# Token combinations of a seven-product pass: from GpSimd in one block to VectorE in eight pieces

## The chip, the cores and the metric

The kernel runs on one core of a Trainium2 chip. The metric is the device time of one execution in microseconds (us); lower is better. Engines are named as in the profile: PE (TensorE), DVE (VectorE), ACT (ScalarE), POOL (GpSimd), and SP, whose queue issues the DMAs.

## The reference

Eight batches of 576 tokens pass through Nystrom attention (8 heads of 64, 32 landmarks, an inverse found by six iterations) and then, all 4608 tokens, through a gated feed-forward layer with 512 inputs and 1536 hidden columns:

```
A, Bm, C = sm(q, k_lm), sm(q_lm, k_lm), sm(q_lm, k)
Z = 2 * Z - Z @ Bm @ Z            # six times
x = (A @ Z @ C @ v)               # heads side by side: 4608 x 512
xn = x / rms(x) * rms_g
out = (silu(xn @ w_gate) * (xn @ w_val)) @ w_out
```

## The kernel before

**Precision.** PE multiplies in a rounded 32-bit format, so operands are kept as a high part (a rounding copy, `Mhi`, `an[:,0]`, `h[:,0]`, `Bhi`) and a low part (the remainder, `Mlo`, `an[:,1]`, `h[:,1]`, `Blo`). A product takes three matmuls: high by high, high by low, low by high.

**Stage 1 (to about 514 us).** The hidden columns are halved into 12 blocks of 128; six (three pairs of gate and value blocks) belong to stage 1. For each batch i (a "chunk"), `mlp` makes 144 matmuls into the banks `psg` and `psv`, ACT takes the silu of one (L469, `s`), DVE multiplies with the other (L470, `s`), ACT makes the high part `h` (L474) and DVE the low part (L475); then `outs` adds the products of `h` with the output weights into `pso` and stores partial results. Into this stream of matmuls a `Mixer` slots the attention of later batches at fixed counts of matmuls: the two `front`s (one for each group of four heads) of batch i+2 (scores `sC` and `sA`, row maxima `mx` L576 to L579, exponentials `E` L582 and `eb` L586, transposes `tA`, landmark sums `lmT` L538), the steps of the inverse (matmuls `pn`, DVE `PV` L838 and `VF` L836), its weights (`W`, `WT`), and `second(b)` for batch i+1, which ends attention: its last piece scales the tokens (DVE `AT` L943), splits them (ACT `an` L945, DVE `an` L946), and forms what the seven-product pass will need.

**Token combinations.** For stage 2 each batch's tokens, cut in a 2 x 2 block of (feature half, token half), are written to the DRAM buffer `ad` as seven blocks with high and low part: three are blocks of `an`, four are differences. Before the change POOL makes the four differences (`tb`, L950 to L953), ACT their high parts in one cast (`thi`, L954), POOL the low parts in one subtraction of 128 x 1152 (L955), and two DMAs store them (L960, L961).

**Stage 2 (514 to 850 us).** For each batch `seven` makes for its six hidden blocks f the seven products of a fast 2 x 2 block scheme (`p<-xb,Bhi` and `p<-xb,Blo`): `step(f, n)` is product n, 12 matmuls, and what follows it on ACT and DVE (`u`, `vv`, `s`); `gate0`, `gate1` and `split` make `s` and `h` from them, on POOL for f up to 4 and on DVE for the last. `outs` for the other half of the output weights follows. `mix_blocks` prepares a pair's weights: two PSUM banks of mixed weights (`pM`) are summed to seven blocks, split into `Bhi` on ACT and `Blo` on DVE (three blocks, `lo1`) and POOL (four, `lo2`, L321). The last two products of a pass are issued inside `outs`, through the list `ends`.

**What sets the order.** Each engine runs its instructions in the order in which the program's scheduler puts them, with `tc.high_priority()` and `issue_after` moving a few; a wait blocks everything behind it on the same engine, and SP's DMA issues stand in one order too. Buffers come from tagged pools: a new tile of a tag waits for all readers of the tile whose slot it takes. `tb` and `thi` share the tag `sq`.

Of the kernel before, what the change touches and what calls it, by code (L numbers as in the profile page):

```python
# [55 lines left out]
def nystrom_moe_kernel(  # L56
# [237 lines left out]

    def mix_blocks(b, pair, banks):

        ps = mixed_banks(late, b, pair, banks)

        def sums():
            homes = HOMES[pair % NPAIR]  # L300
            hi = wp.tile([P, 7, 2, P], F32R, name="Bhi", tag=homes[0])
            if (b, pair) == (0, NPAIR + 1):
                lo1, lo2 = (mp.tile([P, n, 2, P], F32R, name=f"Blo{n}", tag="wraw", bufs=RAWS) for n in (3, 4))
            else:
                lo = wp.tile([P, 7, 2, P], F32R, name="Blo", tag=homes[1])
                lo1, lo2 = lo[:, :3], lo[:, 3:]
            s = lq.tile([P, 4, 2, P], F32, name="S7", tag="lraw", bufs=4)
            both = [p.rearrange("p (i z n) -> p z i n", i=2, z=2) for p in ps]
            a11, a21 = both[0][:, 0], both[0][:, 1]
            a12, a22 = both[1][:, 0], both[1][:, 1]  # L310
            kept(nc.scalar.copy(s[:, 2], a21))
            kept(nc.vector.tensor_add(s[:, 0], s[:, 2], a22))
            kept(nc.scalar.copy(hi[:, 0], a11))
            kept(nc.vector.tensor_sub(s[:, 1], s[:, 0], a11))
            kept(nc.vector.tensor_sub(s[:, 2], a11, s[:, 2]))
            kept(nc.scalar.copy(hi[:, 1:3], both[1]))
            kept(nc.vector.tensor_sub(s[:, 3], a12, s[:, 1]))
            kept(nc.vector.tensor_sub(lo1[:, 0], a11, hi[:, 0].bitcast(F32)))
            kept(nc.scalar.copy(hi[:, 3:], s))  # L319
            kept(nc.vector.tensor_sub(lo1[:, 1:3], both[1], hi[:, 1:3].bitcast(F32)))  # L320
            silu["mix"] = kept(nc.gpsimd.tensor_sub(lo2, s, hi[:, 3:].bitcast(F32)))  # L321
            blocks7[b, pair] = hi, lo1, lo2

        return sums

# [11 lines left out]

    later = []

# [7 lines left out]
    def seven(b, xb, between):  # L347
# [28 lines left out]
        def gate1(f):  # L376
# [3 lines left out]
            kept(eng.tensor_mul(s[:, 1], s[:, 1], vv[f][:, 1]))  # L380

        def gate0(f):
            kept(nc.vector.tensor_mul(ss[f][:, 0], ss[f][:, 0], vv[f][:, 0]))
# [7 lines left out]
        def step(f, n):  # L391
# [7 lines left out]
            elif n == 5:  # L399
                kept(nc.vector.tensor_copy(u[:, 2], p1))  # L400
                kept(nc.vector.tensor_add(v_[:, 1], u[:, 2], p7))
                if last:
# [3 lines left out]
            elif n == 2:  # L406
                kept(nc.vector.tensor_add(s[:, 0], u[:, 0], p2))
                if f > 1:
# [17 lines left out]
        for f in range(NF1):  # L426
            yield from between(f)
            new(f)
            second = ((1, 5), (0, 2)) if f > 1 else ((0, 2), (1, 5))
            for d, n in ((0, 1), *second, (0, 7), (0, 6), (1, 3), (1, 4)):  # L430
                if f >= d:
                    yield from step(f - d, n)
        yield from step(NF1 - 1, 5)
        ends.extend(step(NF1 - 1, n) for n in (3, 4))

# [42 lines left out]
    def outs(wts, b, f0, store, part, following, n0, after=2 * NF1):  # L478
# [5 lines left out]
        for at in range(0, len(groups), 2):  # L484
# [3 lines left out]
            for i, (t, n) in enumerate(order):  # L488
# [9 lines left out]
                yield MMO  # L498
                if ends:
                    yield from ends.pop(0)  # L500
# [13 lines left out]
    with tc.tile_pool(name="ap", bufs=1, side="right") as ap, tc.tile_pool(  # L514
# [180 lines left out]
        def rest(b, inverse, at):  # L695
# [27 lines left out]
            for n in range(6):  # L723
                yield from until(*next(at))
                with tc.high_priority():
                    newton_step(b, n)
                yield 0.45, 0.0
            yield from until(*next(at))
# [5 lines left out]
            for _ in range(4):  # L734
# [3 lines left out]
                if took:  # L738
                    yield took[0], 0.0
            stage["second"] = b  # L740

# [152 lines left out]
        def second(b):  # L894
# [49 lines left out]
            for g in range(2):  # L944
                nc.scalar.copy(an[:, 0, g], ATs[g])  # L945
                fixed["an", b] = nc.vector.tensor_sub(an[:, 1, g], ATs[g], an[:, 0, g].bitcast(F32))  # L946
            tb = ap.tile([P, 4, HS], F32, name="tb", tag="sq", bufs=2)
            thi = ap.tile([P, 4, HS], F32R, name="thi", tag="sq", bufs=2)
            (b11, b12), (b21, b22) = ((a[:, :HS], a[:, HS:]) for a in ATs)
            nc.gpsimd.tensor_sub(tb[:, 0], b12, b11)  # L950
            nc.gpsimd.tensor_sub(tb[:, 2], b22, b12)
            nc.gpsimd.tensor_sub(tb[:, 1], b22, tb[:, 0])
            nc.gpsimd.tensor_sub(tb[:, 3], b21, tb[:, 1])  # L953
            nc.scalar.copy(thi, tb)  # L954
            nc.gpsimd.tensor_sub(tb.bitcast(F32R), tb, thi.bitcast(F32))  # L955
            to = a_dram[b].rearrange("p (a n s) -> p a n s", a=2, n=7)
            af = an.bitcast(F32)
            nc.sync.dma_start(to[:, :, 0], af[:, :, 0, :HS])
            nc.sync.dma_start(to[:, :, 1:3].rearrange("p a n s -> p a (n s)"), af[:, :, 1])
            nc.sync.dma_start(to[:, 0, 3:], thi.bitcast(F32))  # L960
            nc.sync.dma_start(to[:, 1, 3:], tb)  # L961
            ans[b] = an

        hold = ctx.enter_context(ExitStack())
# [173 lines left out]
    def between(b, f):  # L1138
        if b == 0 and f == 1:
            later.append(mix_blocks(0, NPAIR + 2, (pg, "pg")))  # L1140
            yield 1.1
        if b == 0 and f == 2:
            later.pop(0)()

# [44 lines left out]
```

## Time and profile before

| | before |
|---|---|
| median of 3 runs | 851.82 us (851.22 to 851.9) |
| the profiled execution | 851.5 us, of which the span of the trace is 849.6 |
| PE, DVE busy | 801.3 us (94%), 605.3 us (71%) |
| ACT, POOL busy | 414.1 us (49%), 286.7 us (34%) |
| mean granted clock of PE | 0.968 of full speed |

PE is busy for all but 48.3 us of the span. A row of a timeline gives start, duration, engine, line, operation and tile, and in brackets the idle time of its engine before it with what ended that wait; "issue" there means that the profile shows no releaser.

### The profile page before, as it was taken

The page shows a single profiled execution, that of the slowest core. Times are in us where ns is not written, and L with a number is a line of the kernel's source. Part 1 is how long each engine was busy: PE and PEld are TensorE (multiplying, and loading weights), DVE is VectorE, ACT ScalarE, POOL GpSimd, SP SyncE. Part 2 cuts the span into 40 slices and gives each one's busy share as a digit, 9 for nine tenths or more (in the row PEclk, how much of TensorE's full clock was granted, in tenths as well). Part 3 has the DMA queues.
Part 4 walks back from the last instruction along what each step waited for, and adds up shares of the span by engine and source line. Part 5 has one row for each costly group of instructions (what it writes and reads, how often), then busy time and mean ns, then how long its engine had stood idle before and what let it go on. Part 6 is the DMA issues. An engine that isn't in the chain of part 4 may idle for free.

```text
span 849.6 us, 17802 instructions
## 1 busy us (share of the span) xinstructions
PE 801.3 (94%) x7012; PEld 629.9 (74%) x7012; DVE 605.3 (71%) x1295; ACT 414.1 (49%) x899; POOL 286.7 (34%) x274
## 2 busy tenths in 40 slices
PE   7878989899899899899899899899999999999997
PEld 5565657777678578578678587778788787979796
DVE  7999985856867847858857395767666757666662
ACT  4557555435345435435355485545455535444450
POOL 1034450320320411412303114555355535553650
PEclk9877989999999899999999999999999999999999
DMA  9855552350440620621345551052423233242412
GB/s 323 291 179 205 152 207 83 121 195 14 154 162 2 234 94 2 234 82 38 136 128 165 191 172 64 1 179 88 142 107 103 111 112 111 87 148 75 160 39 74
DMA packets 47715, 109.68 MB, mean 129 GB/s; under 512 B 4624, under 2 KB 19984, under 8 KB 47632
## 3 DMA queue, kind: packets, MB, share of 16 engines
q1 hardware_dynamic: 47632, 108.55, 37.3%
q8 instruction: 55, 0.90, 0.4%
q14 instruction: 28, 0.23, 0.1%
HBM read 73.14 MB, written 35.39 MB: 128 GB/s over the span
## 4 chain that ended last, share of the span: by engine, by line
PE 78%; DVE 6%; issue 5%; DMA 5%; ACT 3%; POOL 2%; SPq 0%; DVEq 0%; POOLq 0%; ACTq 0%
PE pso L111 32%; PE p L111 15%; PE psg L111 8%; PE psv L111 8%; PE pM L111 5%; DMA wrawv<-in_moe_w_val_dram 2%; PE pn L111 2%; PE sC L111 2%; PE pCV L111 1%; PE pss L111 1%; PE pO L111 1%; PE sA L111 1%; DMA wrawo<-in_moe_w_out_dram 1%; DMA xb<-ad 1%; DVE wgv L185 1%
## 5 line engine op out<-in xcount | busy, mean ns | idle before, releaser
L111 PE MATMUL pso<-wo,h 128*128 128x512 f32 x648 | 164.9, 407 | 3.0 <-DVE h L475 2.0
L111 PEld LDWEIGHTS pso<-wo,h 128*128 128x128 f32 x648 | 122.4, 194 | 37.8 <-issue 3.4
L111 PE MATMUL p<-xb,Bhi 128*128 128x288 f32 x672 | 139.7, 302 | 4.8 <-ACT u L396 3.8
L111 PE MATMUL pso<-lhio,h 128*128 128x512 f32 x432 | 140.2, 393 | 0.7 <-ACT h L387 0.5
L111 PEld LDWEIGHTS p<-xb,Bhi 128*128 128x128 f32 x672 | 107.4, 188 | 15.4 <-ACT u L396 6.9
L111 PEld LDWEIGHTS pso<-lhio,h 128*128 128x128 f32 x432 | 81.0, 188 | 24.7 <-issue 5.9
L111 PE MATMUL p<-xb,Blo 128*128 128x288 f32 x336 | 98.9, 294 | 0.0
L111 PE MATMUL psg<-an,Mhi 128*128 128x288 f32 x384 | 87.0, 310 | 5.3 <-ACT s L469 3.3
L111 PE MATMUL pso<-lloo,h 128*128 128x512 f32 x216 | 84.3, 390 | 0.0
L111 PE MATMUL psv<-an,Mhi 128*128 128x288 f32 x384 | 84.1, 303 | 0.0
L321 POOL TENSOR_TENSOR Blo<-S,Bhi 128x1024 fp32r<-128x1024 f32 x24 | 57.7, 2404 | 61.6 <-ACT Bhi L319 61.6
L111 PEld LDWEIGHTS psg<-an,Mhi 128*128 128x128 f32 x384 | 63.1, 193 | 18.5 <-ACT h L474 5.0
L389 POOL TENSOR_TENSOR h<-s,h 128x576 fp32r<-128x576 f32 x40 | 59.0, 1474 | 37.2 <-ACT h L387 37.2
L111 PEld LDWEIGHTS psv<-an,Mhi 128*128 128x128 f32 x384 | 62.9, 191 | 2.1
L111 PEld LDWEIGHTS p<-xb,Blo 128*128 128x128 f32 x336 | 63.1, 188 | 0.0
L469 ACT ACTIVATE s<-psg 128x288 f32<-128x288 f32 x96 | 39.5, 412 | 47.2 <-PE psg L111 46.9
L475 DVE TENSOR_TENSOR h<-s,h 128x576 fp32r<-128x576 f32 x48 | 51.5, 1072 | 12.8 <-ACT h L474 12.7
L111 PE MATMUL psv<-an,Mlo 128*128 128x288 f32 x192 | 59.0, 308 | 0.0
L111 PE MATMUL psg<-an,Mlo 128*128 128x288 f32 x192 | 58.9, 307 | 0.0
L387 ACT CAST h<-s 128x576 fp32r<-128x576 f32 x48 | 32.3, 672 | 54.5 <-POOL s L380 31.8
L1047 ACT COPY ob<-pso 128x512 f32<-128x512 f32 x36 | 21.1, 589 | 75.2 <-PE pso L111 43.7
L470 DVE TENSOR_TENSOR s<-s,psv 128x288 f32<-128x288 f32 x96 | 42.3, 446 | 20.7 <-PE psv L111 17.2
(172 smaller groups left out, 1558.7 us busy)
## 6 DMA issues: line engine op xcount, KB each, us to landing
xb<-ad SPq DMA_DIRECT2D x16, 1008.0 KB, 5.3
qk<-in_q_dram SPq DMA_DIRECT2D x16, 576.0 KB, 4.7
qk<-in_k_dram SPq DMA_DIRECT2D x16, 576.0 KB, 5.8
pd<-ob SPq DMA_DIRECT2D x36, 256.0 KB, 3.1
obl<-pd SPq DMA_DIRECT2D x36, 256.0 KB, 2.7
out_dram<-obl SPq DMA_DIRECT2D x36, 256.0 KB, 2.2
vt<-in_v_dram SPq DMA_DIRECT2D x16, 512.0 KB, 5.5
wrawg<-in_moe_w_gate_dram SPq DMA_DIRECT2D x12, 512.0 KB, 4.9
```

The source lines that it names most:

```text
L111: tc.keep_in_program_order(nc.tensor.matmul(*args, **kw))
L185: nc.vector.scalar_tensor_tensor(w, w, 3, wtail, op0=ALU.logical_shift_left, op1=ALU.bitwise_or)
L321: silu["mix"] = kept(nc.gpsimd.tensor_sub(lo2, s, hi[:, 3:].bitcast(F32)))
L387: kept(nc.scalar.copy(h[:, 0, TAIL:], s))
L389: kept(eng.tensor_sub(h[:, 1, TAIL:], s, h[:, 0, TAIL:].bitcast(F32)))
L469: silu["last"] = nc.scalar.activation(s[:, cols], banks[0], AF.Silu).ins
L470: nc.vector.tensor_mul(s[:, cols], s[:, cols], banks[1])
L475: gated[b, f0 // NF1, 2 * n + i] = nc.vector.tensor_sub(h[:, 1, TAIL:], s, h[:, 0, TAIL:].bitcast(F32))
L1047: nc.scalar.copy(ob, ps)
```

## The change

Three things are edited.

1. In `second(b)` the four POOL differences, the ACT cast, the POOL subtraction and the two 576 KB stores go. A generator `token_blocks` makes the same blocks as eight DVE instructions of 128 x 288 (four differences, L1000 of the changed kernel, and four low parts, L1005), four ACT casts of 128 x 288 (L1004) and eight stores of 144 KB (L1007). Its four pieces are taken one by one behind the steps of the **next** batch's inverse; those of the last batch right behind its own `an`. The tiles `t` come from the tag `tA` with three slots, so the fourth difference takes the slot of the first one, and waits for its two stores.
2. `mix_blocks` can hand out its sums in six pieces. Only batch 0's third pair uses that: a piece is taken behind each product n = 7 and n = 4 (f = 1 to 3), where before all sums came at the start of f = 2.
3. In each pass the addition `s = u + p2` of f = 1 is made right behind the copy of `u` for f = 0's product 5 (`first0`), and the two products in `ends` are issued one group of three `pso` matmuls later.

```
--- before.py
+++ after.py
@@ -292,11 +292,11 @@
     HOMES = [("wgv0", "wgv1"), ("wgv2", "wo0"), ("wo1", "wo2")]
     blocks7 = {}
 
-    def mix_blocks(b, pair, banks):
+    def mix_blocks(b, pair, banks, whole_pair=True):
 
         ps = mixed_banks(late, b, pair, banks)
 
-        def sums():
+        def sums(whole=True):
             homes = HOMES[pair % NPAIR]
             hi = wp.tile([P, 7, 2, P], F32R, name="Bhi", tag=homes[0])
             if (b, pair) == (0, NPAIR + 1):
@@ -308,20 +308,46 @@
             both = [p.rearrange("p (i z n) -> p z i n", i=2, z=2) for p in ps]
             a11, a21 = both[0][:, 0], both[0][:, 1]
             a12, a22 = both[1][:, 0], both[1][:, 1]
+            blocks7[b, pair] = hi, lo1, lo2
+
+            def high(n):
+                kept(nc.scalar.copy(hi[:, n], (a11, a12, a22)[n]))
+
+            def low(n):
+                kept(nc.vector.tensor_sub(lo1[:, n], (a11, a12, a22)[n], hi[:, n].bitcast(F32)))
+
             kept(nc.scalar.copy(s[:, 2], a21))
             kept(nc.vector.tensor_add(s[:, 0], s[:, 2], a22))
-            kept(nc.scalar.copy(hi[:, 0], a11))
+            yield
+            high(0)
             kept(nc.vector.tensor_sub(s[:, 1], s[:, 0], a11))
+            yield
             kept(nc.vector.tensor_sub(s[:, 2], a11, s[:, 2]))
-            kept(nc.scalar.copy(hi[:, 1:3], both[1]))
+            if whole:
+                kept(nc.scalar.copy(hi[:, 1:3], both[1]))
+            else:
+                high(1)
+            yield
             kept(nc.vector.tensor_sub(s[:, 3], a12, s[:, 1]))
-            kept(nc.vector.tensor_sub(lo1[:, 0], a11, hi[:, 0].bitcast(F32)))
-            kept(nc.scalar.copy(hi[:, 3:], s))
-            kept(nc.vector.tensor_sub(lo1[:, 1:3], both[1], hi[:, 1:3].bitcast(F32)))
+            if not whole:
+                high(2)
+            yield
+            low(0)
+            for n in (slice(0, 4),) if whole else (slice(0, 2), slice(2, 4)):
+                if n.start:
+                    yield
+                kept(nc.scalar.copy(hi[:, 3 + n.start : 3 + n.stop], s[:, n]))
+                if not whole:
+                    low(1 + n.start // 2)
+            if whole:
+                kept(nc.vector.tensor_sub(lo1[:, 1:3], both[1], hi[:, 1:3].bitcast(F32)))
             silu["mix"] = kept(nc.gpsimd.tensor_sub(lo2, s, hi[:, 3:].bitcast(F32)))
-            blocks7[b, pair] = hi, lo1, lo2
-
-        return sums
+
+        def at_once():
+            for _ in sums():
+                pass
+
+        return at_once if whole_pair else sums(False)
 
     def load_x(b):
         to = a_dram[b].rearrange("p (a n s) -> p a n s", a=2, n=7)
@@ -335,7 +361,7 @@
     def behind(ins):
         return tc.issue_after(ins) if ins else nullcontext()
 
-    later = []
+    later, pieces = [], []
 
     hs, ends = [], []
 
@@ -379,6 +405,9 @@
             silu["last"] = kept(nc.scalar.activation(s[:, 1], banks[f][0], AF.Silu))
             kept(eng.tensor_mul(s[:, 1], s[:, 1], vv[f][:, 1]))
 
+        def first0(f):
+            kept(nc.vector.tensor_add(ss[f][:, 0], us[f][:, 0], banks[f][1]))
+
         def gate0(f):
             kept(nc.vector.tensor_mul(ss[f][:, 0], ss[f][:, 0], vv[f][:, 0]))
 
@@ -398,13 +427,16 @@
                     gate1(f - 2)
             elif n == 5:
                 kept(nc.vector.tensor_copy(u[:, 2], p1))
+                if f == 0:
+                    first0(1)
                 kept(nc.vector.tensor_add(v_[:, 1], u[:, 2], p7))
                 if last:
                     gate1(f - 1)
                     gate0(f - 1)
                     split(f - 1)
             elif n == 2:
-                kept(nc.vector.tensor_add(s[:, 0], u[:, 0], p2))
+                if f != 1:
+                    first0(f)
                 if f > 1:
                     gate0(f - 2)
             elif n == 6:
@@ -430,6 +462,8 @@
             for d, n in ((0, 1), *second, (0, 7), (0, 6), (1, 3), (1, 4)):
                 if f >= d:
                     yield from step(f - d, n)
+                if pieces and n in (7, 4):
+                    next(pieces[0], None)
         yield from step(NF1 - 1, 5)
         ends.extend(step(NF1 - 1, n) for n in (3, 4))
 
@@ -496,7 +530,7 @@
                 yield MMO
                 mm(bank[t], hs[n][:, 1, sl], hi, start=False, stop=(n == NF1 - 1))
                 yield MMO
-                if ends:
+                if ends and i:
                     yield from ends.pop(0)
                 if n == NF1 - 1:
                     store(t, bank[t], obs.pop(t))
@@ -724,6 +758,7 @@
                 yield from until(*next(at))
                 with tc.high_priority():
                     newton_step(b, n)
+                next(blocks_of[b - 1], None)
                 yield 0.45, 0.0
             yield from until(*next(at))
             with tc.high_priority():
@@ -737,6 +772,9 @@
                     took = next(parts, None)
                 if took:
                     yield took[0], 0.0
+            if b == B - 1:
+                for _ in blocks_of[b]:
+                    yield -0.3
             stage["second"] = b
 
         def steady():
@@ -944,22 +982,41 @@
             for g in range(2):
                 nc.scalar.copy(an[:, 0, g], ATs[g])
                 fixed["an", b] = nc.vector.tensor_sub(an[:, 1, g], ATs[g], an[:, 0, g].bitcast(F32))
-            tb = ap.tile([P, 4, HS], F32, name="tb", tag="sq", bufs=2)
-            thi = ap.tile([P, 4, HS], F32R, name="thi", tag="sq", bufs=2)
-            (b11, b12), (b21, b22) = ((a[:, :HS], a[:, HS:]) for a in ATs)
-            nc.gpsimd.tensor_sub(tb[:, 0], b12, b11)
-            nc.gpsimd.tensor_sub(tb[:, 2], b22, b12)
-            nc.gpsimd.tensor_sub(tb[:, 1], b22, tb[:, 0])
-            nc.gpsimd.tensor_sub(tb[:, 3], b21, tb[:, 1])
-            nc.scalar.copy(thi, tb)
-            nc.gpsimd.tensor_sub(tb.bitcast(F32R), tb, thi.bitcast(F32))
             to = a_dram[b].rearrange("p (a n s) -> p a n s", a=2, n=7)
             af = an.bitcast(F32)
             nc.sync.dma_start(to[:, :, 0], af[:, :, 0, :HS])
             nc.sync.dma_start(to[:, :, 1:3].rearrange("p a n s -> p a (n s)"), af[:, :, 1])
-            nc.sync.dma_start(to[:, 0, 3:], thi.bitcast(F32))
-            nc.sync.dma_start(to[:, 1, 3:], tb)
+            blocks_of[b] = token_blocks(b, ATs, to)
             ans[b] = an
+
+        blocks_of = {}
+
+        def token_blocks(b, ATs, to):
+            (b11, b12), (b21, b22) = ((a[:, :HS], a[:, HS:]) for a in ATs)
+            ts = {}
+
+            def less(n, x, y):
+                ts[n] = ap.tile([P, 2, HS], F32, name=f"t{n}", tag="tA", bufs=TAB)
+                kept(nc.vector.tensor_sub(ts[n][:, 0], x, y))
+
+            def split(n):
+                t = ts[n]
+                nc.scalar.copy(t[:, 1].bitcast(F32R), t[:, 0])
+                kept(nc.vector.tensor_sub(t[:, 0].bitcast(F32R), t[:, 0], t[:, 1]))
+                for a in range(2):
+                    nc.sync.dma_start(to[:, a, 2 + n], t[:, 1 - a])
+
+            less(3, b22, b12)
+            less(1, b12, b11)
+            yield
+            split(3)
+            less(2, b22, ts[1][:, 0])
+            yield
+            split(1)
+            less(4, b21, ts[2][:, 0])
+            yield
+            split(2)
+            split(4)
 
         hold = ctx.enter_context(ExitStack())
 
@@ -1137,10 +1194,8 @@
 
     def between(b, f):
         if b == 0 and f == 1:
-            later.append(mix_blocks(0, NPAIR + 2, (pg, "pg")))
+            pieces.append(mix_blocks(0, NPAIR + 2, (pg, "pg"), False))
             yield 1.1
-        if b == 0 and f == 2:
-            later.pop(0)()
 
     mix.fill(mlp(early, B - 1, 0, ans.pop(B - 1), keep, lambda t: None, first_blocks))
     for b in range(B):
```

**On DVE, at the inverse of batch 6 in chunk 5.** `PV` are the steps of the inverse (L838 before, L876 after), `s` and `h` the gate of the running chunk. Before:

```order
L838 SCALAR_TENSOR_TENSOR PV<-PV,pn 128x192
L470 TENSOR_TENSOR s<-s,psv 128x288
L838 SCALAR_TENSOR_TENSOR PV<-PV,pn 128x192 x2
L470 TENSOR_TENSOR s<-s,psv 128x288
L838 SCALAR_TENSOR_TENSOR PV<-PV,pn 128x192
L475 TENSOR_TENSOR h_754<-s,h_754 128x576
L836 SCALAR_TENSOR_TENSOR VF<-PV,pn 128x128 x2
L470 TENSOR_TENSOR s<-s,psv 128x288 x2
```

The same place in the changed kernel, with buffer numbers (`t_4792` is the third difference, `t_4794` the first, `t_4821` the second, `t_4848` the fourth), up to the fourth difference:

```order
L876 SCALAR_TENSOR_TENSOR PV<-PV,pn 128x192
L1000 TENSOR_TENSOR t_4792<-AT 128x288
L1000 TENSOR_TENSOR t_4794<-AT 128x288
L504 TENSOR_TENSOR s<-s,psv 128x288
L876 SCALAR_TENSOR_TENSOR PV<-PV,pn 128x192
L1005 TENSOR_TENSOR t_4792<-t_4792 128x288
L1000 TENSOR_TENSOR t_4821<-AT,t_4794 128x288
L876 SCALAR_TENSOR_TENSOR PV<-PV,pn 128x192
L1005 TENSOR_TENSOR t_4794<-t_4794 128x288
L504 TENSOR_TENSOR s<-s,psv 128x288
L876 SCALAR_TENSOR_TENSOR PV<-PV,pn 128x192
L509 TENSOR_TENSOR h_744<-s,h_744 128x576
```

Behind these rows come the fourth difference (`t_4848`), the two `VF`, the last two low parts, the two `s`, and then `W` and `WT`. The eight new instructions stand between the steps of the inverse, at most two behind one `PV`.

**On ACT, at the end of chunk 5.** Before, the cast `thi` stands ahead of the cast of the chunk's last `h` and of the second front's exponentials (table load, `E`, `eb`):

```order
L945 CAST an<-AT 128x576 x2
L469 ACTIVATE s<-psg 128x288
L954 CAST thi<-tb 128x1152
L474 CAST h_1310<-s 128x576
L582 ACT_TABLE_LOAD
L582 ACTIVATE E,ss<-sC,mx 128x288 x2
```

After:

```order
L983 CAST an<-AT 128x576 x2
L503 ACTIVATE s<-psg 128x288
L508 CAST h_1324<-s 128x576
L616 ACT_TABLE_LOAD
L616 ACTIVATE E,ss<-sC,mx 128x288 x2
```

Only `thi` is gone; nothing takes its place there.

**On POOL, in the first pass of stage 2.** `Blo` is the low part of four blocks of one pair (three pairs), `s` and `h` are gate and split of f = 0, 1, 2. Before:

```order
L321 TENSOR_TENSOR Blo<-S_6428,Bhi 128x1024
L321 TENSOR_TENSOR Blo_6480<-S_6481,Bhi 128x1024
L321 TENSOR_TENSOR Blo<-S_6589,Bhi 128x1024
L380 TENSOR_TENSOR s_6526<-s_6526,vv 128x288
L389 TENSOR_TENSOR h_754<-s_6526,h_754 128x576
L380 TENSOR_TENSOR s_6558<-s_6558,vv 128x288
L389 TENSOR_TENSOR h_896<-s_6558,h_896 128x576
```

After:

```order
L344 TENSOR_TENSOR Blo<-S_6540,Bhi 128x1024
L344 TENSOR_TENSOR Blo_6592<-S_6593,Bhi 128x1024
L406 TENSOR_TENSOR s_6638<-s_6638,vv 128x288
L418 TENSOR_TENSOR h_744<-s_6638,h_744 128x576
L406 TENSOR_TENSOR s_6670<-s_6670,vv 128x288
L418 TENSOR_TENSOR h_886<-s_6670,h_886 128x576
L344 TENSOR_TENSOR Blo<-S_6689,Bhi 128x1024
```

The third pair's `Blo` has moved behind gate and split of the first two blocks.

## Rows read from the trace of the kernel before

**Rows 1.** The page: busy time by engine, share of the span, instructions.

```profile
PE 801.3 (94%) x7012; PEld 629.9 (74%) x7012; DVE 605.3 (71%) x1295; ACT 414.1 (49%) x899; POOL 286.7 (34%) x274
```

**Rows 2.** The chain in time order, chunks 1 and 5: start, us, what.

```profile
166.56 2.27 issue
...
171.34 1.59 PE pso L111 x6
...
398.21 0.93 PE pso L111 x4
...
400.33 6.12 PE pso L111 x26
406.44 2.29 issue
...
411.84 2.56 PE pso L111 x6
```

**Rows 3.** Timelines of DVE, ACT and POOL at the end of chunk 5.

```profile
398.46 2.64 DVE L946 TENSOR_TENSOR an<-AT,an 128x576 fp32r<-128x576 f32 x2
...
403.57 2.77 DVE L475 TENSOR_TENSOR h<-s,h 128x576 fp32r<-128x576 f32 x1 [0.98 <-ACT h L474]
...
407.32 2.57 DVE L538 TENSOR_REDUCE lmT<-qk 128x64 f32<-128x1152 f32 x2
...
401.80 1.16 ACT L954 CAST thi<-tb 128x1152 fp32r<-128x1152 f32 x1 [3.51 <-POOL tb L953]
...
407.02 1.28 ACT L582 ACT_TABLE_LOAD   x1 [3.49 <-DVE mx L579]
...
403.04 2.68 POOL L955 TENSOR_TENSOR tb<-tb,thi 128x1152 fp32r<-128x1152 f32 x1 [1.27 <-ACT thi L954]
```

**Rows 4.** All instructions of L475: duration in ns, min/median/max.

```profile
L475 DVE TENSOR_TENSOR h<-s,h x48: 717/753/2766, 55.7 to 511.1; 128x576 fp32r<-128x576 f32 x48
```

**Rows 5.** Windows: PE, PEld, DVE, ACT, POOL busy, PEclk, DMA share, GB/s.

```profile
406.00:410.00 4.00, 1.10 (x6) 0.20 (x6) 4.00 (x10) 2.63 (x7) 0.00 (x0) 1.00 0.37 147
410.00:414.00 4.00, 4.00 (x44) 2.93 (x44) 3.54 (x13) 0.55 (x2) 0.33 (x1) 0.57 0.00 0
```

**Rows 6.** Timelines of PE and DVE at the end of chunk 6.

```profile
468.48 0.73 PE L111 MATMUL pso<-wo,h 128*128 128x512 f32 x2 [1.01 <-ACT h L474]
471.22 1.49 PE L111 MATMUL pso<-wo,h 128*128 128x512 f32 x4 [2.01 <-DVE h L475]
472.63 1.96 PE L111 MATMUL pM<-wgv,WT 64*32 64x512 f32 x16
...
468.46 2.71 DVE L475 TENSOR_TENSOR h<-s,h 128x576 fp32r<-128x576 f32 x1 [2.98 <-ACT h L474]
```

**Rows 7.** Timelines in chunk 0: ACT, PE, DVE.

```profile
111.21 1.15 ACT L954 CAST thi<-tb 128x1152 fp32r<-128x1152 f32 x1 [2.92 <-POOL tb L953]
...
114.32 1.17 PE L111 MATMUL sC<-qk,lmT 64*32 64x288 f32 x2 [1.15 <-ACT E L582]
...
49.50 3.12 DVE L188 SCALAR_TENSOR_TENSOR wgv<-wrawg,wgv 128x512 int32<-128x512 int32 x1
```

**Rows 8.** DVE timeline through the inverse in chunk 5.

```profile
434.29 0.35 DVE L838 SCALAR_TENSOR_TENSOR PV<-PV,pn 128x192 f32<-128x192 f32 x1
435.19 0.45 DVE L470 TENSOR_TENSOR s<-s,psv 128x288 f32<-128x288 f32 x1 [0.54 <-PE psv L111]
435.88 0.35 DVE L838 SCALAR_TENSOR_TENSOR PV<-PV,pn 128x192 f32<-128x192 f32 x1 [0.24 <-PE pn L111]
```

**Rows 9.** DMA issues by tile: count, KB each, us from issue to landing.

```profile
ad<-an SPq DMA_DIRECT2D x8, 288.0 KB, 2.8
```

**Rows 10.** The first pass of stage 2: timelines of PE and POOL.

```profile
537.73 0.54 PE L111 MATMUL p<-xb,Bhi 128*128 128x288 f32 x2 [1.86 <-ACT u L396]
...
541.89 0.53 PE L111 MATMUL p<-xb,Bhi 128*128 128x288 f32 x2 [0.64 <-ACT u L396]
...
537.46 2.40 POOL L321 TENSOR_TENSOR Blo<-S,Bhi 128x1024 fp32r<-128x1024 f32 x1 [7.90 <-ACT Bhi L319]
```

## The prediction

> **What bounds the kernel now.** I read the page first: PE is busy for 801.3 of 849.6 us [rows 1], no other engine for more than 71%. So the time is PE's own work plus the stretches in which PE waits, and the change, which gives PE no more and no less to multiply, can only act through those 48.3 us and through what a wait does to PE's clock. Next I followed the chain that ended last, to see where PE waits: the same place returns in chunks 1 to 5, at the second front. In chunk 5 PE ends its `pso` products at 406.44, is idle for 2.29 us, makes the first two `sC`, waits again, and is back at `pso` at 411.84 [rows 2]. The first front of the same batch, the same work with nothing to wait for, took from 399.14 (398.21 + 0.93) to 400.33, 1.19 us [rows 2].
>
> Then I looked at what the other engines did in those microseconds [rows 3]. DVE makes `h` (L475) in 2.77 us; the same instruction has a median of 0.753 and a minimum of 0.717 [rows 4]. It runs from 403.57 while POOL's subtraction of 128 x 1152 runs from 403.04 to 405.72, and ends at 406.34, 0.62 us after that. `an`, beside POOL's differences, takes 2.64 us for two, while two at the shortest would take about 1.45 (twice L475's 0.72, the same shape and kind). And `h` started late: ACT's high part of `h` stands behind the cast `thi`, which waited 3.51 us for POOL's differences. Behind `h` come the first group's row maxima, then ACT's table load at 407.02 (idle 3.49 us for `mx`) and the exponentials, and DVE's `lmT`, 407.32 to 409.89; PE's second front needs both. So the stall is made by the token combinations: once through the queue on ACT, once through DVE's slowness beside POOL.
>
> By the Trainium skill ("SBUF — State Buffer", Who interferes with whom) a DVE instruction with two SBUF inputs and a GpSimd instruction that reads SBUF exclude each other for their whole length. By that rule `h` would end at 405.72 + 0.72 = 406.44; the trace has 406.34, so it agrees, and bears on the first rival below.
>
> **Term 1: second fronts of chunks 1 to 5.** What the stall costs is the time from the end of `pso` to the next `pso`, less 1.19, and what the lowered clock adds to the next six `pso` (26 took 6.12 us, so six take 1.41). Chunk 5: 411.84 - 406.44 - 1.19 = 4.21, and 2.56 - 1.41 = 1.15: 5.4 us. Chunk 1: 171.34 - 166.56 - 1.19 = 3.59, and 0.18: 3.8 [rows 2]. Chunks 2 to 4, worked out alike, give 4.8, 6.5 and 5.3. Sum 25.8. The granted clock is 1.00 in the 4 us around the idle time, and 0.57 in the 4 us after it [rows 5]: what is lost to the clock follows the wait, and goes with it.
>
> Does all of it go? With POOL silent, and `thi` gone, in chunk 5: `an` ends near 399.9 instead of 401.1 (1.45 for 2.64), two `s`, `mx` and `tA` take DVE to about 401.5; ACT makes its part of `h` by 401.3, DVE its own by 402.3, the maxima follow to about 403.0, `lmT` takes 2.57 as before, to 405.6; ACT's table load (1.28) and exponentials end near 405.3. PE arrives at 406.44. Margin 0.8 us: the whole stall goes. If I am 1 us wrong in every chunk, 0.2 to 1 us of it comes back in each. **25.8**, bounds 21 and 26.
>
> **Term 2: end of chunk 6.** PE waits 1.01 us for ACT's `h` and 2.01 for DVE's (2.71 long) [rows 6]. Behind it four `pso` take 1.49 us (0.94 at 6.12 for 26) and the 16 `pM` 1.96 (twice the 1.0 that they take elsewhere at full clock). Sum 4.5. Here the last batch's own eight instructions stand around this `h`: six DVE instructions at 0.45 ahead of what follows it, two or four of them ahead of `h` itself, some 1.8 us, in place of POOL's 4 us; I put `h` at 466.5 to 467, PE needs it from 467.47. **4.5**, bounds 2 and 5.
>
> **Term 3: chunk 0.** At 111.21 `thi` stands ahead of the table load, waiting 2.92 us for POOL; PE waits at 114.32 for `E` [rows 7]. The cast ends at 112.36, and the table load follows; without it the load waits for `mx` alone, at about 108.7 by the shorter `an`: 3.7 us earlier, `lmT` (2.57 long, to about 111.3) and `E` are both there by 111.4, and I add 0.6 for a clock that I expect to recover only partly. Earlier in chunk 0 DVE's work stands without idle time and POOL's combinations lengthen it by about 4 us, as I read it (one weight instruction of 3.12 us [rows 7] carries 2.4 of them); 3.6 us of new work come back in the next inverse. Net 1.3. **5.6**, bounds 3 and 8.
>
> **Term 4: the new instructions.** Per batch eight DVE instructions of 128 x 288. The trace has no such subtraction with POOL silent; the nearest row is `s`, the same size, 0.45 us [rows 8]: 3.6 us a batch, for 7 batches in the next inverse. Its steps are 1.59 us apart (434.29, 435.88) and PV takes 0.35; with two new instructions and an `s` behind a PV there are 0.35 + 0.9 + 0.45 = 1.70, 0.1 too many, elsewhere 1.25. The idle time there is 0.54 and 0.24 in one step [rows 8]. Bounds 0 (all in idle time) and 3.6 a batch (none); I take 0.15, nearer to the first by the idle rows: **-1.0**, bounds 0 and -7 (1 us a batch). The four ACT casts, about 0.4 each by size, lie in idle ACT time (49% busy). Behind the new instructions on DVE stand `VF`, `s`, `W` and `WT`, and PE waits for those.
>
> The fourth difference waits for the stores of the third block. In the times of the trace, the third's low part would end at 435.88 + 0.35 + 0.45 = 436.7; a store of 288 KB lands in 2.8 us [rows 9], so the slot is free at 439.5, and the fourth difference stands behind a PV of about 439.1 and an `h` of 0.75: 440.2. No wait, margin 0.7.
>
> By the Trainium skill ("DMA: Bandwidth & Descriptors", Anatomy of one DMA) each DMA pays about 2.0 us fixed, whatever its size, which speaks against eight small stores in place of two. By its fit 144 KB take about 2.3 us (an estimate), and 288 KB 2.7 against 2.8 in the trace; no row here shows stores of 144 KB. The slot would be free at 439.0, and the sum is the same, unless the stores run one behind the other (third rival).
>
> **Term 5: third pair of batch 0.** PE's idle time in the first pass, 1.86, 0.64 and two of 0.22, 2.9 us in all, is laid to the sums made in one block [rows 10]. Spread out, each piece sits ahead of some `u`, `vv` or silu for which the next product waits; I count four waits of 0.45 to 0.7, 2.5 us. And POOL's `Blo` now stands behind the second block's split: cast, 1.4 us of split, 2.40 us of `Blo` [rows 10], while the third block's products come; that I put at 3.2. Net **-2.8**, bounds -5 and +2.9.
>
> **Term 6.** The shifted `ends` and `first0`: single waits of 0.1 to 0.2 us a pass. **-0.6**, bounds -1.6 and +1.
>
> **Sum.** 25.8 + 4.5 + 5.6 - 1.0 - 2.8 - 0.6 = 31.5. 851.5 - 31.5 = 820.0, for a profiled execution 0.3 below the median of the runs shown, so 820 stands for either.
>
> **Rivals.**
> *The stall goes only by half*: what delays the front is DVE's own queue, and the next in line (`lmT`, `E`) ends 2.5 us late in each chunk. For it: the margin of 0.8 us comes out of a chain of seven durations. Against: L475's length, and POOL's end 0.62 us before its end. 820 + 13 = 833.
> *DVE becomes the bound in the inverse*: 3.6 us a batch, half of them not hidden, 7 batches: 12.6 - 1.0 more, 832. Against: the idle time in [rows 8], and DVE's 71% of the span [rows 1].
> *Stores one behind the other*: the third block's second store is the third in the queue. At 2.3 us each (which the page gives), or 2.8 each as in [rows 9], it lands near 442.5 to 444; the fourth difference, and DVE behind it, waits 2.3 to 3.7 us in six batches, 14 to 22 us: 834 to 842.
> *Slower*: the same wait, if a store takes so long that PE loses more than the 31.5 us: from 5.3 us in each of six batches, a landing of about 8.8 us instead of 2.8. At 7 us: 862. Against: [rows 9].
> *The third pair's spreading gains*: its stall goes, 2.9 instead of -2.8, and chunk 0 is at its upper bound: 812.
>
> **How the numbers follow.** Forecast (815 to 827) 0.62; spreading gains 0.12; half 0.09; DVE bound 0.07; stores 0.05; within 0.2% (1.7 us, about what a measurement of this kernel can tell from no change) 0.02; slower 0.03. The predicted time is 820. The range 811 to 834 leaves out the slower cases, most of the store rival and a rest of the best one, together under 0.2.
>
> **What would show it.** In the changed profile: no idle PE before the second `sC` of chunks 1 to 5, six `pso` behind it in about 1.41; L475 at a maximum under 1 us; `an` near 0.72; the clock at 1.00 there. Term 4 is wrong if PE waits for `PV`, `VF` or `W`, or if the fourth difference has idle time before it; term 5 is right if PE waits in the first pass for `Blo` of the third pair. The prediction falls if PE's waits at the fronts stay, with DVE or ACT busy with something else.

## The result and the profile after

| | before | after |
|---|---|---|
| median | 851.52 us (4 runs) | 819.36 us (4 runs, 819.07 to 819.86) |
| ratio to before | | 0.9625, 95% interval 0.9608 to 0.9641 |
| span of the profiled execution | 849.6 us | 818.1 us |
| mean granted clock | 0.968 | 0.985 |

Faster by 32 us, with 820 forecast. The page's first part, against [rows 1]: PE has 19 us less busy time for the same 7012 matmuls, POOL 60 us less. PE's idle time went from 48.3 to 35.9 us; so of the 31.5 us by which the span is shorter, 12.4 are waits that are gone, and 19.1 are time that the matmuls themselves no longer take.

```profile
PE 782.2 (96%) x7012; PEld 623.8 (76%) x7012; DVE 598.0 (73%) x1360; ACT 418.1 (51%) x925; POOL 226.4 (28%) x234
```

The chain at the second fronts of chunks 1 and 5, against [rows 2] (start, us, what):

```profile
157.00 6.12 PE pso L111 x26
...
164.30 1.59 PE pso L111 x6
...
375.05 0.93 PE pso L111 x4
...
377.16 6.12 PE pso L111 x26
...
384.46 1.59 PE pso L111 x6
```

No idle time stands between the 26 `pso` (to 383.28) and the next six: the second front takes 1.18 us, as the first one does (375.98 to 377.16). Chunk 5's six `pso` take 1.59 instead of 2.56; I had forecast 1.41, but chunk 1 took 1.59 before too. How a wait also lengthens the matmuls behind it shows in the kernel before: the same `sC` in the first front of chunk 5 and, behind the stall, in the second, where [rows 5] has a clock of 0.57.

```profile
399.61 0.40 PE L111 MATMUL sC<-qk,lmT 64*32 64x288 f32 x1
...
410.51 0.68 PE L111 MATMUL sC<-qk,lmT 64*32 64x288 f32 x1
```

Timelines of DVE and ACT at the end of chunk 5, against [rows 3]:

```profile
374.67 1.42 DVE L984 TENSOR_TENSOR an<-AT,an 128x576 fp32r<-128x576 f32 x2
...
377.56 0.76 DVE L509 TENSOR_TENSOR h<-s,h 128x576 fp32r<-128x576 f32 x1
...
379.30 2.57 DVE L572 TENSOR_REDUCE lmT<-qk 128x64 f32<-128x1152 f32 x2
...
376.85 0.67 ACT L508 CAST h<-s 128x576 fp32r<-128x576 f32 x1 [1.72 <-DVE s L504]
...
379.01 1.28 ACT L616 ACT_TABLE_LOAD   x1 [1.49 <-DVE mx L613]
...
381.44 0.20 ACT L620 ACTIVATION_READ_ACCUMULATOR eb<-sC,mx 128x1 f32 x1
```

`an` takes 1.42 for 2.64, `h` 0.76 for 2.77, and ACT's part of `h` waits for DVE's `s` and no longer behind `thi`. `lmT` ends at 381.87 and `eb` at 381.64; PE comes at 383.28, a margin of 1.4 us in this chunk. The clock in the windows there, against [rows 5] (the column behind POOL):

```profile
380.00:384.00 4.00, 4.00 (x45) 2.91 (x48) 2.47 (x6) 1.63 (x7) 0.00 (x0) 1.00 0.00 0
384.00:388.00 4.00, 4.00 (x50) 2.35 (x35) 3.88 (x14) 2.35 (x9) 1.24 (x2) 1.00 0.18 66
```

The end of chunk 6, timelines of PE and DVE, against [rows 6]: `pso` run through, `h` is done at 438.66, and the fourth difference waits 2.90 us for the stores of the third block, with nothing behind it that PE needs soon.

```profile
432.30 8.35 PE L111 MATMUL pso<-wo,h 128*128 128x512 f32 x36
440.57 1.09 PE L111 MATMUL pM<-wgv,WT 64*32 64x512 f32 x16
...
437.90 0.76 DVE L509 TENSOR_TENSOR h<-s,h 128x576 fp32r<-128x576 f32 x1
...
441.94 0.46 DVE L1000 TENSOR_TENSOR t<-AT,t 128x288 f32<-128x288 f32 x1 [2.90 <-DMA ad<-t]
```

Both traces hold all 7012 matmuls. But for `sC` and `sA` inside the second fronts, and the shifted products in `ends` in stage 2, they stand in one order. So what was gained up to a place is read from the same matmul in both: its start before less its start after is the "lead" of the changed kernel there.

| matmul | before | after | lead |
|---|---|---|---|
| a `pM` of the opening, after 42 us | 42.28 | 43.32 | -1.0 |
| `pso` behind the second front of chunk 0 (timeline) | 116.32 | 114.77 | 1.6 |
| the same, chunk 1 (chain) | 171.34 | 164.30 | 7.0 |
| the same, chunk 5 (chain) | 411.84 | 384.46 | 27.4 |
| two batches of `pM` at the end of stage 1 | 513.70 | 480.47 | 33.2 |
| 48 `pM` behind the first pass of stage 2 | 593.66 | 562.88 | 30.8 |
| last `pso` | 845.46 | 813.98 | 31.5 |

### The profile page after: what moved, and what is told of

Its sections match the earlier page's. It is cut to its first block, busy times and chain, and to the rows that moved or that the text cites. A ratio compares the mean times of both kernels' runs of the same rounds, so it can differ in the third digit from the quotient of the medians.

```text
span 818.1 us, 18012 instructions
## 1 busy us (share of the span) xinstructions
PE 782.2 (96%) x7012; PEld 623.8 (76%) x7012; DVE 598.0 (73%) x1360; ACT 418.1 (51%) x925; POOL 226.4 (28%) x234
## 4 chain that ended last, share of the span: by engine, by line
PE 83%; DVE 8%; issue 3%; ACT 2%; DMA 2%; POOL 1%; SPq 0%; DVEq 0%; POOLq 0%; ACTq 0%
PE pso L111 36%; PE p L111 14%; PE psg L111 9%; PE psv L111 9%; PE pM L111 5%; PE pn L111 2%; PE sC L111 2%; PE pCV L111 1%; PE pss L111 1%; PE pO L111 1%; DMA qk<-in_k_dram 1%; DMA vl<-in_vl_dram 1%; PE sE L117 1%; PE pW L111 1%; DVE u L429 0%
## 5 line engine op out<-in xcount | busy, mean ns | idle before, releaser
L111 PE MATMUL pso<-wo,h 128*128 128x512 f32 x648 | 158.5, 396 | 0.8 <-DVE s L504 0.8
L111 PEld LDWEIGHTS pso<-wo,h 128*128 128x128 f32 x648 | 118.6, 188 | 32.4 <-ACT E L616 4.2
L111 PEld LDWEIGHTS p<-xb,Bhi 128*128 128x128 f32 x672 | 109.2, 190 | 12.1 <-ACT u L425 2.8
L649 POOL TENSOR_TENSOR tA<-tA,mA 128x576 f32<-128x576 f32 x16 | 18.8, 1194 | 169.0 <-DVE mA L648 169.0
L1165 DVE TENSOR_TENSOR obl<-obl,pso 128x512 f32<-128x512 f32 x36 | 24.6, 684 | 40.6 <-PE pso L111 40.5
```

Source lines behind the costliest of these rows:

```text
L111: tc.keep_in_program_order(nc.tensor.matmul(*args, **kw))
L649: nc.gpsimd.tensor_sub(tA, tA, mA.unsqueeze(2).broadcast_to([P, NB, M]))
L1165: kept(nc.vector.tensor_add(ob, ob, ps))
```

## The experiments

Times are medians; "lead" is read as in the table, for the same matmuls.

**The token combinations alone.** The changed kernel with edits 2 and 3 undone.

```
-            pieces.append(mix_blocks(0, NPAIR + 2, (pg, "pg"), False))
+            later.append(mix_blocks(0, NPAIR + 2, (pg, "pg")))
...
-                if ends and i:
+                if ends:
...
+                first0(f)
```

Expected: 

> Only the token combinations are changed (pieces on VectorE behind the next inverse); the third pair's sums, first0 and ends are as before. Theory, by the ledger of PE's checkpoints in the two traces (lead of the changed kernel 33.2 us at the end of stage 1, 30.8 after the first pass, 31.5 at the end): the combinations are worth 33.2, the other two edits lose 1.7 together. So 851.5 - 33.2 = 818.3. Rival: the other edits help the gain somewhere in stage 1 or take nothing: 819.4 or above.

Measured: 815.61 us, ratio 0.9578 (0.9564 to 0.9593). Its lead at the end of stage 1 is 35.1 against 33.2, and the 1.9 between them are there at 51 us, where nothing differs yet between the two versions (last section). After the first pass it is still 35.2, and 36.0 at the end. So the combinations make all of the gain, and the rise of 0.8 over the later passes, which I had put down to the other edits, is there without them.

**The other edits alone.** The token combinations as before.

Expected: 

> The token combinations as before on GpSimd; the third pair's pieces, first0 and the shifted ends as in the change. Theory: stage 1 unchanged, first pass of stage 2 2.4 us longer, 0.7 back over the later passes: 851.5 + 1.7 = 853.2. Rival, the edits help where the stalls of the fronts are still there: 851 or less.

Measured: 852.83 us, ratio 1.002 (1.0008 to 1.0032). The sign is the theory's: the lead falls by 1.7 in the first pass (1.1 to -0.6), where I had put 2.4. No gain is left without the token combinations.

**The third pair as before, all else changed.**

Expected: 

> The change without the third pair's pieces (its sums at the start of f = 2 as before), with the token pieces, first0 and ends. Theory: the 2.29 us wait for Blo of the third pair and four small waits go, the waits of before (1.86, 0.64 and two of 0.22) come back: 819.4 - 2.4 = 817.0. Rival: the wait moves elsewhere in the first pass, 819 to 820.

Measured: 817.54 us, ratio 0.9601 (0.9583 to 0.962). The lead through the first pass goes from 33.4 to 32.8; with the pieces it went from 33.2 to 30.7: by the lead the pieces lose 2.0. Timeline of PE in the first pass of the changed kernel, against [rows 10]:

```profile
499.87 0.54 PE L111 MATMUL p<-xb,Bhi 128*128 128x288 f32 x2 [0.91 <-DVE s L409]
...
505.06 0.53 PE L111 MATMUL p<-xb,Bhi 128*128 128x288 f32 x2 [0.55 <-DVE vv L451]
506.59 0.54 PE L111 MATMUL p<-xb,Bhi 128*128 128x288 f32 x2 [0.47 <-ACT s L405]
507.90 0.85 PE L111 MATMUL p<-xb,Bhi 128*128 128x288 f32 x2 [0.65 <-DVE s L409]
514.93 0.40 PE L111 MATMUL p<-xb,Blo 128*128 128x288 f32 x1 [2.29 <-POOL Blo L344]
```

The same place in the version with the third pair as before:

```profile
499.72 0.53 PE L111 MATMUL p<-xb,Bhi 128*128 128x288 f32 x2 [0.91 <-DVE s L409]
505.01 0.54 PE L111 MATMUL p<-xb,Bhi 128*128 128x288 f32 x2 [1.85 <-ACT u L425]
```

So the first of the four short waits, 0.91, is not the pieces'. The other three (1.7 us) and the one for POOL's `Blo` (2.29) take the place of 2.7 (1.85, 0.64 and 0.22): 1.3 us more of idle time, and the rest of the 2.0 is longer matmuls.

**first0 alone beside the token combinations.** One execution, read by the lead.

```
+                if f == 0:
+                    first0(1)
...
-                first0(f)
+                if f != 1:
+                    first0(f)
```

Expected: 

> The token combinations with first0 (s of f = 1 made behind the copy of u for f = 0's product 5), with the ends and the third pair as before. In the first pass the change waits 0.91 us for that s where the kernel before waits 0.22. If the earlier place of s makes that, PE loses 0.7 us in the first pass here; if the ends do, nothing: read from the lead of PE's instructions in the trace, since it is less than a measurement can tell.

Measured: 816.21 us; the lead falls from 34.9 to 34.2 in the first pass, and PE waits 0.91 for `s` there. So the 0.7 is `first0`'s; by the lead, the shifted `ends` change nothing beyond 0.1 us (the version above, which has both, loses 0.6).

**The pieces on GpSimd, at the same place.**

```
-                kept(nc.vector.tensor_sub(ts[n][:, 0], x, y))
+                kept(nc.gpsimd.tensor_sub(ts[n][:, 0], x, y))
```

and the same for the low parts. Expected: 

> The change with the eight subtractions of a batch on GpSimd, at the same places behind the next inverse. Theory, that the place matters more than the engine: the fronts of chunks 1 to 5 keep their gain; the last batch's pieces stand at the end of chunk 6 as before, so some 5 us come back there, and some 1 to 2 us by VectorE being slowed beside GpSimd in the inverses: 825 to 828. Rival, that the gain came from the change of engine: the cost of GpSimd beside VectorE moves with it into the inverses, 835 or more.

Measured: 837.26 us, ratio 0.9827 (0.9809 to 0.9846). The rival's number, but not its reason. The idle time at the second fronts of chunks 1 to 5 is gone, and the longest `h` (L509) takes 1.8 us, much as in the changed kernel (1.6). What is lost shows in the timelines of ACT and PE in the inverse that runs in chunk 5:

```profile
413.48 0.43 ACT L1004 CAST t<-t 128x288 fp32r<-128x288 f32 x1 [2.27 <-POOL t L1000]
...
418.88 0.59 ACT L1104 COPY ob<-pso 128x512 f32<-128x512 f32 x1 [4.00 <-DMA pd<-ob]
...
419.52 0.40 PE L111 MATMUL psv<-an,Mhi 128*128 128x288 f32 x1 [2.05 <-ACT ob L1104]
```

The fourth piece's cast stands on ACT ahead of the copies `ob` that empty PE's banks, and waits for POOL, which waits 1.01 us for the third block's stores. So two copies, and their stores `pd<-ob`, go out late, and the next copy waits 4.00 us for one of these stores. PE waits 1.0 to 2.9 us for `ob` at six places, one in each of chunks 1 to 6. By the lead this version loses 17.7 us in the stretches from one second front to the next and up to the end of chunk 6, where the changed kernel loses 0.2. So what stood behind the pieces in the queues decided. That POOL also takes 0.8 us for a subtraction where DVE takes 0.45 adds to it, and was not tested by itself.

**The pieces on VectorE, but in place.**

```
-                next(blocks_of[b - 1], None)
...
-            blocks_of[b] = token_blocks(b, ATs, to)
+            for _ in token_blocks(b, ATs, to):
+                pass
```

Expected: 

> The change, with all eight VectorE instructions of a batch issued right behind its own an, not behind the next inverse. Theory, that the place decides: in chunk 5 of the changed kernel the landmark sums end at 381.9 and PE comes to the front at 383.3; 3.6 us more on VectorE ahead of them take the 1.4 us of margin and leave PE waiting some 2 us in each of chunks 1 to 5, and the clock falls again behind it in some: 819.4 + 10 to 16 = 829 to 835. Rival, that only leaving GpSimd matters: 819 to 821.

Measured: 835.82 us, ratio 0.9801 (0.9783 to 0.9818), at the upper end of the theory. The place is worth as much as half of the gain: PE waits some 0.3 us ahead of `sC` and 1.17 ahead of `sA` in each second front of chunks 1 to 5, and the lead behind chunk 0 is 4.8 us smaller. PE in chunk 5:

```profile
397.22 0.64 PE L111 MATMUL sC<-qk,lmT 64*32 64x288 f32 x2 [0.33 <-issue]
399.03 0.40 PE L111 MATMUL sA<-qk,lmT 64*32 64x288 f32 x1 [1.17 <-issue]
```

**Only the cast and the low part later**, on the kernel before.

```
+            def low(after=None):
+                with tc.issue_after(after) if after else nullcontext():
+                    nc.scalar.copy(thi, tb)
+                nc.gpsimd.tensor_sub(tb.bitcast(F32R), tb, thi.bitcast(F32))
+                nc.sync.dma_start(to[:, 0, 3:], thi.bitcast(F32))
+                nc.sync.dma_start(to[:, 1, 3:], tb)
...
+                if n == 0:
+                    held.pop(b - 1)(fixed["eb", b, 1].ins)
```

Expected: 

> The kernel before, with only the cast thi, GpSimd's subtraction of 128 x 1152 and the two stores moved behind the second front's exponentials (but for the last batch); the four differences stay on GpSimd beside an. Theory, that the stall has two parts, the queue on ACT behind thi and h slowed beside that subtraction: both go, an stays slow (1.2 us of the margin), so most of chunks 1 to 5 comes back, 20 to 25 us, nothing at the end of chunk 6, 2 to 4 in chunk 0, and the cast and subtraction cost 1 to 3 us where they are now: 825 to 831. Rival, that the differences beside an make the stall: 845 or more.

Measured: 827.09 us, ratio 0.9703 (0.9685 to 0.9721). PE has no idle time over 0.3 us at the second fronts of chunks 1 to 5, and a lead of 22.3 at the end of stage 1. DVE at the end of chunk 5:

```profile
380.72 2.63 DVE L948 TENSOR_TENSOR an<-AT,an 128x576 fp32r<-128x576 f32 x2
...
384.83 0.76 DVE L475 TENSOR_TENSOR h<-s,h 128x576 fp32r<-128x576 f32 x1
...
386.57 2.57 DVE L538 TENSOR_REDUCE lmT<-qk 128x64 f32<-128x1152 f32 x2
```

`an` is as slow as before; `h` is quick and early, `lmT` ends at 389.14 and the 26 `pso` at 388.71 (382.52 + 6.19). So the differences beside `an` cost the margin, and the two moved instructions the stall.

**Only the low part later**, `thi` left in its place, behind the first step of the next inverse; further down the same with its store queued last.

Expected: 

> The kernel before, with only GpSimd's subtraction of 128 x 1152 and its store moved into the next inverse (but for the last batch); the cast thi stays where it is. Theory, that the two parts add: h is quick (0.75 instead of 2.77) but still late behind thi, so 2 us of idle time go in each of chunks 1 to 5 and some of the clock's loss; some 1.5 to 2 us of idle time stay: 10 to 16 us, and 1 to 3 in chunk 0: 833 to 840. Rival A, that the queue on ACT alone makes the stall: 849 to 852. Rival B, that the slow h alone makes it: 826 or less.

Measured: 846.22 us (841.21 to 849.08), ratio 0.9907 (0.9871 to 0.9943): outside what I had put for the theory and both rivals. PE's wait at chunk 5's second front is 0.28 + 0.62 instead of 2.29 + 0.62: 2.0 us, as forecast. But in three chunks PE waits 2.05 to 2.49 us in the inverse, for `ob`. Timelines of SP and ACT:

```profile
421.47 0.32 SPq L966 DMA_DIRECT2D ad<-tb  x1
421.88 1.46 SPq L157 DMA_DIRECT2D wrawg<-in_moe_w_gate_dram  x2
423.43 1.10 SPq L1060 DMA_DIRECT2D pd<-ob  x2
...
430.04 0.59 ACT L1059 COPY ob<-pso 128x512 f32<-128x512 f32 x1 [7.29 <-DMA pd<-ob]
```

The store `ad<-tb` waits on SP for POOL until 421.5; the weight loads go out behind it and right ahead of `pd<-ob`, which takes 6.5 us, and ACT waits for its buffer. In the kernel before these loads go out at 416.20, 11 us ahead of that `pd<-ob` (427.10).

```
+            def put():
+                with tc.issue_after(fixed["pd"].ins) if "pd" in fixed and b < B - 1 else nullcontext():
+                    nc.sync.dma_start(to[:, 1, 3:], tb)
...
+                if n in (0, 4):
+                    held[b - 1][n // 4]()
```

Expected: 

> As the run in which only GpSimd's subtraction of 128 x 1152 was moved into the next inverse, but with its store queued on SP behind the stores of the partial results. Theory: in that run the front's stall lost its 2 us in each chunk, and three to four chunks lost 2 to 2.5 us again in the inverse, because the weight loads stood on SP behind the waiting store and then ran beside a store of partial results, for whose buffer ACT waited. With the store last these waits go: 846.2 - 6 = 838 to 842. Rival, that the waits come from GpSimd's subtraction beside the inverse itself: 845 to 848.

Measured: 834.95 us, ratio 0.9802 (0.9788 to 0.9815), below the 838 to 842 of the theory. The waits for `ob` are gone; the fronts keep 0.28 + 0.62, here in chunk 5:

```profile
392.79 0.64 PE L111 MATMUL sC<-qk,lmT 64*32 64x288 f32 x2 [0.28 <-issue]
394.05 0.40 PE L111 MATMUL sA<-qk,lmT 64*32 64x288 f32 x1 [0.62 <-issue]
```

So the queue on SP cost 11 us, more than I had put, and moving the low part alone is worth 17 us. With the cast moved too it was 25: the slow `h` beside POOL is the larger part of the stall, and the queue behind `thi` adds 8 us by the medians, 5 by the lead at the end (23.1 against 18.0). No run moves the cast alone.

**Batch 0's pieces two steps later**, the token combinations alone otherwise.

```
+                if b > 1 or n > 1:
+                    next(blocks_of[b - 1], None)
```

Expected: 

> The token combinations alone (as in the first of these runs), with batch 0's pieces behind steps 2 to 5 of batch 1's inverse instead of 0 to 3. Theory, that the 3.64 us for which PE waits in chunk 0 for VectorE's s come from two pieces and the order that they bring (s behind the second AT, which waits for GpSimd): s is ahead of it here, 2 to 4 us less: 812 to 814. Rival, that VectorE is full there anyway and the wait moves: 815 to 816.

Measured: 814.0 us, ratio 0.9549 (0.9533 to 0.9564). In chunk 0 of the changed kernel PE waits 4.38 us at 79.00 (3.64 in the version with the combinations alone). Timelines of DVE and PE there:

```profile
76.86 0.78 DVE L663 STREAM_TRANSPOSE AT<-tA 128x576 f32<-128x576 f32 x1 [1.05 <-POOL tA L661]
77.56 0.65 DVE L188 SCALAR_TENSOR_TENSOR w<-wrawo,w 128x512 int32<-128x512 int32 x1
78.13 0.45 DVE L1000 TENSOR_TENSOR t<-AT 128x288 f32<-128x288 f32 x1
78.50 0.45 DVE L504 TENSOR_TENSOR s<-s,psv 128x288 f32<-128x288 f32 x1
...
79.00 0.61 PE L111 MATMUL psv<-an,Mhi 128*128 128x288 f32 x1 [4.38 <-DVE s L504]
```

`s` stands behind an `AT` that waits for POOL, and behind a piece. With the pieces later, `s` stands ahead of that `AT`, and PE waits 0.57 there; the lead behind it is 3.7 instead of 1.0 with the combinations alone. Some comes back as new waits of 1.0 to 1.4 us later in the chunk, and 1.4 us remain of it behind the second front.

**The fourth difference in a slot of its own**, on that version.

```
+                    ts[n] = ap.tile([P, 4, HS], F32, name="t4", tag="sq", bufs=2)[:, :2]
```

Expected: 

> The fastest version so far (token combinations alone, batch 0's pieces two steps later, 814.0) with the fourth difference in a slot of another tag, so that it waits for no store of the third block. Theory: the two waits that VectorE had for it (0.78 us in batch 6, 2.9 at the end of chunk 6) were hidden, PE waited for nothing behind them: 813.5 to 814.5. Rival, that these waits, and shorter ones under the trace's notice, cost time: 811 or less.

Measured: 814.84 us, ratio 0.9574 (0.9561 to 0.9587). DVE has no wait for a store there any more, and nothing is gained (814.0 with the waits): they were hidden.

## Why the prediction was right, point by point

- **Term 1** (second fronts of chunks 1 to 5): 25.8 forecast, 24.9 measured, from chunk 0's 3.4 (lead at the next batch's `psg`) to 28.4 behind chunk 5's six `pso` (27.4 + 2.56 - 1.59). By chunks it is 3.6, 4.6, 6.3, 5.2 and 5.2, each some 0.2 under the forecast: the six `pso` take 1.59 at the full clock and not 1.41. Of the 24.9, 14.0 are idle time and 10.9 matmuls that no longer run long. The margin in chunk 5 was 1.4 us, not 0.8. The runs that move the cast and the low part, the low part alone, or only the place of the new pieces show the mechanism: the slow `h` and the queue behind `thi` make the stall, and 3.6 us in the wrong place on DVE bring part of it back. One sign failed: the longest `h` takes 1.64 us and not under 1, once, in chunk 0 beside POOL's `tA`.
- **Term 4** (the new instructions): -1.0 forecast. In chunks 1 to 5 they cost PE nothing, the lead between one second front and the next changes by 0.01 us at most; in chunk 6 it falls by 0.2 (28.4 to 28.2). They take 0.45 us each, as estimated; DVE in chunk 1:

```profile
130.31 0.36 DVE L876 SCALAR_TENSOR_TENSOR PV<-PV,pn 128x192 f32<-128x192 f32 x1
130.58 0.45 DVE L1005 TENSOR_TENSOR t<-t 128x288 fp32r<-128x288 f32 x1
130.95 0.45 DVE L1000 TENSOR_TENSOR t<-AT,t 128x288 f32<-128x288 f32 x1
131.89 0.35 DVE L876 SCALAR_TENSOR_TENSOR PV<-PV,pn 128x192 f32<-128x192 f32 x1 [0.49 <-PE pn L111]
```

  It still waits for PE there. In chunk 0, where DVE has no such idle time, they did cost (term 3). Of the third rival (stores one behind the other) the trace shows two waits of the fourth difference, 0.78 and 2.90 us, where I had put none, and the last run that they cost nothing; a store of 144 KB lands in 2.1 us. By the Trainium skill ("DMA: Bandwidth & Descriptors", Anatomy of one DMA), whose fit is of DMAs that GpSimd issues, while SP issues these, it would be about 2.3 (an estimate), and the trace nearly agrees. Eight stores instead of two show nowhere in PE's time: in the changed kernel PE has no wait over 0.3 us from 114 to 460 us.
- **Term 2**: 4.5 forecast, 5.0 measured (28.2 to 33.2).
- **Term 3**, chunk 0: 5.6 forecast, 3.4 measured. This is the term that was mis-sized, in both of its parts. The second front gave 5.5 (lead -2.1 to 3.4) for 4.3. The part ahead of it lost 2.1, where I had put a gain of 1.3; and that 1.3 does not follow from its own figures, since 4 us less 3.6 of new work is 0.4. The early gain was there: in the trace before, between 45 and 70 us, the lead rises from -1.0 to 4.5. It rises by 2.7 over the stretch of [rows 7]'s slowed weight instruction, and by 3.0 at this wait of the kernel before, which is gone:

```profile
69.93 0.85 PE L111 MATMUL psg<-an,Mhi 128*128 128x288 f32 x2 [2.90 <-ACT s L469]
```

  But the new pieces brought an order on DVE by which PE waited 4.38 us, and I had counted only their 3.6 us of work. How much of the miss is the opening shows the version with the combinations alone, the same program in chunk 0: there PE waits 3.64 us, the lead behind chunk 0 is 5.5, near the forecast, and 1.9 of the 2.1 between the two stand at 51 us. But for the opening, then, the 5.6 holds by two opposite errors, 1.2 more at the front and 1.3 less ahead of it.
- **Term 5**: -2.8 forecast, -2.0 measured by the lead; the wait for `Blo` was 2.29 and not 3.2, and three short waits took 1.7 against four of 2.5 (the fourth, 0.91, is `first0`'s).
- **Term 6**: -0.6 forecast; `first0` loses 0.6 to 0.7 in the first pass, and what the later passes gain (0.7) is not the edits', since the combinations alone have it too.

The sum: 24.9 - 0.2 + 5.0 + 3.4 - 2.4 (first pass, 33.2 to 30.8) + 0.7 = 31.4, with rounding 31.5. The mechanism was right, but that 820 was met so closely is luck: terms 1 and 3 gave 3.1 us less than forecast, terms 2, 4, 5 and 6, with the later passes, 3.0 more.

## What to carry to other kernels

Before moving work off a slow engine, look at what stands behind it in the other queues: here a subtraction that ran beside `h` cost 17 us, a cast that waited on ACT 5 to 8, and, in one version, a store that waited on SP 11, and the same pieces gave 32, 16 or 14 us by their place and engine. Moving work into a latency-bound stretch pays where the engine idles between steps; where it doesn't (chunk 0), ask what order the new pieces force on the old ones. An edit that spreads work to remove a wait should be timed alone: the third pair's pieces and `first0` lost 2.6 us inside a change that gained 32; the best version leaves them out.

## What the runs showed of the hardware that was not expected

The clock of the opening differs between the traces of versions in which nothing yet differs. Windows of the changed kernel, then of the token combinations alone (the clock behind POOL's column):

```profile
28.00:32.00 4.00, 3.05 (x33) 2.69 (x30) 3.92 (x7) 1.00 (x2) 0.00 (x0) 0.72 1.09 362
32.00:36.00 4.00, 3.88 (x39) 2.39 (x38) 2.92 (x6) 1.62 (x5) 0.00 (x0) 0.85 0.71 227
...
48.00:52.00 4.00, 4.00 (x25) 3.95 (x25) 3.32 (x6) 1.56 (x4) 0.00 (x0) 0.72 0.87 274
```

```profile
28.00:32.00 4.00, 3.04 (x42) 2.50 (x34) 4.00 (x8) 0.87 (x2) 0.00 (x0) 1.00 1.10 356
32.00:36.00 4.00, 3.69 (x57) 1.81 (x65) 3.97 (x8) 2.83 (x9) 0.00 (x0) 1.00 0.77 259
...
48.00:52.00 4.00, 4.00 (x38) 3.73 (x44) 3.44 (x7) 2.12 (x5) 0.00 (x0) 1.00 0.77 247
```

The changed kernel has 0.72 and 0.85 from 28 to 36 us, and its lead falls by 1.3 us there; the other has 1.00, and its lead stays. The rest comes from 44 to 52 us, where the clock is again lower in the changed kernel (0.72 against 1.00 from 48 us). At the `psg` that stands at 50.86 us before, the lead is 0.2 against 2.1 us. So differences of 1 to 2 us between two versions are read from the leads behind the opening, not from single spans. What sets the opening's clock was not settled, nor whether it goes with the execution or with the version: there is one trace of each, and the four times of the two (819.07 to 819.86, 815.39 to 816.37) do not overlap.
